# Cutting the last loads of a decode kernel differently: values in two pieces, down weights in four

## The chip, the cores and the metric

The kernel runs on one core of a Trainium2 chip. The metric is device time in microseconds (us) of the whole program, lower is better. A profile is one execution; its span is a little shorter than the device time (512.7 us against about 514.3 us), because it counts from the first to the last recorded instruction. Engines: PE is the matrix engine (PEld its weight loads), DVE the vector engine, ACT the scalar engine, POOL is GpSimd, and SP is the engine that issues nearly all loads.

## The reference, cut to what matters

One token goes through attention and MLP, and then through both once more with the same weights and the same cache. Attention reads the last 4,096 keys and values of 32 heads of width 192; the MLP is 640 to 1,536 and back.

```python
def _A_ref(x, k_cache, v_cache, wq, wo):
    W = min(4096, max(256, Sk // 4))                     # 4096
    q = ... x @ wq ...
    scores = jnp.einsum("bhqd,bhkd->bhqk", q, k) * (Dh ** -0.5)
    p = _softmax(scores, axis=-1)
    o = jnp.einsum("bhqk,bhkd->bhqd", p, v)
    return ... o @ wo
def _B_ref(x, w_gate, w_up, w_down):
    g = x @ w_gate; u = x @ w_up                          # cut: einsums
    return (_sigmoid(g) * u) @ w_down
x = x + _A_ref(_layernorm(x), ...)
x = x + _B_ref(_layernorm(x), ...)
# the same two lines once more
```

For a single token this is a job of moving bytes: 218 MB of cache and weights for a few matrix-vector products.

## The kernel before

Keys and values come in head pairs, through seven slots of on-chip memory. `seq` is the order of loads; SP issues each as soon as its slot is free, so loads are mostly queued well ahead of the compute (about 20 us at the end). The last cache load of a layer is that of the values of one head pair (12,288 columns of 2 bytes on 128 partitions; the first half is head 0, the second head 1). It was cut in three: head 1 as `b1` (in layer 1 with the output weights behind it), then head 0 as two quarters. The matmuls of head 1 run first, then those of each quarter.

```python
def last_values(l, p):
    return [("b1", l, p), ("b0", l, p, 0), ("b0", l, p, 1)]
...
elif k == "b1":
    n, o1 = len(pg.ops["dma"]), UNIT if it[1] else VE
    pg.dma(q_dma(slot(s, NB * DH, o1 - NB * DH), b_in(it[2], NB * DH, o1)), f"b1_{it[1]}", wr=[rslot[s]])
elif k == "b0":
    o = it[3] * NHALF                                     # NHALF: a quarter, 3072 columns
    pg.dma(q_dma(slot(s, o, NHALF), b_in(it[2], o, o + NHALF)), f"bh{it[3]}", wr=[res(f"bh{it[3]}")], extra=ev_done["b1"])
```

In layer 1 the gate, up and down weights of the last MLP follow at once. `finish` ends the program: up projection, then the down projection, whose weights come in `WFIN` pieces, each with its own semaphore.

```python
WFIN = [(0, 6), (6, 10), (10, 12)]                        # blocks of 128 rows of w_down
...
nc.all_engine_barrier()                                   # line 882
finish()                                                  # of which, after the up projection:
for i_, (c0, c1) in enumerate(WFIN):
    if i_ < 2:
        nc.tensor.wait_ge(tail_sem["copy"], i_ + 1)
    for c in range(c0, c1):
        for g in range(NRG):                              # 4 column groups of the PE array
            i = nc.tensor.matmul(yrow[32 * g:32 * g + 1, 0:RW], lhsT=hT[:, c:c + 1],
                                 rhs=slot(D_SLOT, c * D + g * RW, RW), ..., tile_position=(0, 32 * g))
            if c == c0 and g == 0:
                i._wait_ge(tail_sem[f"d:wf{i_}"], 16)
i.then_inc(tail_sem["row"], 1)
nc.vector.tensor_copy(out=o_row[...], in_=yrow[...])._wait_ge(tail_sem["row"], 3).then_inc(tail_sem["copy"], 1)
```

## Time and profile before

| what | before |
|---|---|
| device time, median of the first three runs | 514.38 us (514.02 to 514.49) |
| span of the profile | 512.7 us |
| bytes loaded, mean rate | 218.71 MB, 427 GB/s |
| last landing of a load | 510.05 us |
| last landing to start of the closing copy | 0.53 us |

The head of the profile's page. The rows in tenths give the busy share of each of 40 slices, the GB/s row what the load engines moved in each:

```profile
span 512.7 us, 8581 instructions
...
PE 263.9 (51%) x3716; PEld 138.7 (27%) x3716; DVE 100.3 (20%) x379; ACT 85.0 (17%) x171; POOL 4.2 (1%) x31
...
DMA  9999999999999999999999999999999999999996
GB/s 431 426 423 426 427 430 428 430 461 439 426 430 426 435 430 426 443 457 430 394 420 415 419 438 441 434 425 425 461 439 435 426 426 430 445 426 417 427 429 273
DMA packets 9964, 218.71 MB, mean 427 GB/s; under 512 B 1240, under 2 KB 1368, under 8 KB 4952
```

The load engines are busy in every slice but the last, and no compute engine is busy for much over half the time. What can be won is overhead of transfers, or work left over when the last byte has landed. That work is in the chain of waits (start us, length, what), here of the last microseconds:

```profile
485.35 24.70 DMA big<-in_wd_dram
510.05 0.04 issue
510.10 0.46 PE o L748 x6
510.56 0.02 issue
510.58 0.33 DVE o_sb L754
```

The last down-weight load was issued at 485.35 and landed at 510.05; then come eight matmuls (the chain counts six of them), the copy out of PSUM, and the store. The timeline around the last values of layer 1 (start us, length, engine, line, what; in brackets the idle time before it and what ended it):

```profile
492.69 0.82 PE L487 MATMUL o<-big,et_sb 128*2 128x384 bf16 x16
494.45 0.65 PE L487 MATMUL o<-big,et_sb 128*2 128x384 bf16 x8 [0.94 <-DMA big<-in_uc_dram]
496.30 0.81 PE L487 MATMUL o<-big,et_sb 128*2 128x384 bf16 x8 [1.20 <-DMA big<-in_uc_dram]
...
500.86 1.76 PE L674 MATMUL scores<-sh,big 128*128 128x1 bf16 x60 [0.40 <-DVE sc L372]
505.74 1.07 PE L735 MATMUL scores<-sh,big 128*128 128x1 bf16 x35 [1.82 <-PEq L882]
507.81 0.97 PE L748 MATMUL o<-big,sh 128*1 128x160 bf16 x24 [0.33 <-DMA big<-in_wd_dram]
...
510.09 0.10 PEld L748 LDWEIGHTS o<-big,sh 128*1 128x1 bf16 x8 [0.41 <-DMA big<-in_wd_dram]
```

Head 1 runs at 492.69, the two quarters of head 0 at 494.45 and 496.30, each on its landing. Then the gate projection starts at 500.86, the up projection at 505.74, the down projection at 507.81. The last eight weight loads of PE, at 510.09, wait for the last down-weight piece.

The windows view near the end shows how the load stream runs out (time, length, busy time of PE, PEld, DVE, ACT, POOL, granted PE clock, busy share of the load engines, GB/s):

```profile
507.00:508.00 1.00, 0.67 (x26) 0.58 (x27) 0.30 (x2) 0.00 (x0) 0.00 (x0) 0.50 0.71 289
508.00:509.00 1.00, 0.78 (x24) 0.43 (x16) 0.00 (x0) 0.00 (x0) 0.00 (x0) 0.50 0.48 188
509.00:510.00 1.00, 0.67 (x16) 0.36 (x16) 0.00 (x0) 0.00 (x0) 0.00 (x0) 0.50 0.16 61
```

The sixteen load engines don't finish together (the last load has sixteen landing records, from 507.31 to 510.05 us): the rate falls over three microseconds, and the last of them sets the landing.

### The profile page before, as it was taken

Reading aid. Unit: us, or ns where it says so; the run is one execution under the profiler, and the core shown is the slowest. Engines: PE = TensorE matmul, PEld = TensorE weight load, DVE = VectorE, ACT = ScalarE, POOL = GpSimd, SP = SyncE. Lnnn points to the kernel's source line nnn. Section 1 sums busy time; section 2 is a strip of 40 time slices with the busy share of each in tenths; the row PEclk is TensorE's granted clock in tenths of the full one; section 3 lists DMA queues with packets and bytes.
Section 4 is the critical chain, followed back from the end, with each engine's and each line's share of the span. In section 5 each row is a group of like instructions: output and inputs, shape, how many; then the busy total and the mean of one; then the engine's idle time right before and its main releaser. Section 6 shows DMA issues by size and latency. Waiting matters only on the chain.

```text
span 512.7 us, 8581 instructions
## 1 busy us (share of the span) xinstructions
PE 263.9 (51%) x3716; PEld 138.7 (27%) x3716; DVE 100.3 (20%) x379; ACT 85.0 (17%) x171; POOL 4.2 (1%) x31
## 2 busy tenths in 40 slices
PE   0362455344643254445565777774625344634665
PEld 0221222122312122222234434532312122312334
DVE  0221212112210121112121243321202111210311
ACT  1110111011110111011120024130301011101220
POOL 0010000000000000000000000000000000000000
PEclk9955665566565775556575568765755566556565
DMA  9999999999999999999999999999999999999996
GB/s 431 426 423 426 427 430 428 430 461 439 426 430 426 435 430 426 443 457 430 394 420 415 419 438 441 434 425 425 461 439 435 426 426 430 445 426 417 427 429 273
DMA packets 9964, 218.71 MB, mean 427 GB/s; under 512 B 1240, under 2 KB 1368, under 8 KB 4952
## 3 DMA queue, kind: packets, MB, share of 16 engines
q1 hardware_dynamic: 9800, 218.37, 99.1%
q8 instruction: 13, 0.21, 0.1%
q10 hardware_dynamic: 144, 0.06, 0.0%
q14 instruction: 7, 0.06, 0.0%
HBM read 218.43 MB, written 0.00 MB: 426 GB/s over the span
## 4 chain that ended last, share of the span: by engine, by line
DMA 63%; PE 24%; DVE 7%; ACT 3%; SPq 2%; issue 2%; DVEq 0%; POOL 0%; ACTq 0%; POOLq 0%
DMA big<-in_uc_dram 54%; PE scores L430 8%; PE o L487 7%; DMA big<-in_wd_dram 6%; DMA big<-in_wu_dram 3%; DVE sc L440 3%; PE bank L446 2%; SPq L214 2%; PE bank L412 2%; ACT e_sb L454 2%; PE bank L522 1%; PE bank L460 1%; ACT diag L443 1%; DVE sc L472 1%; DVE qs L418 1%
## 5 line engine op out<-in xcount | busy, mean ns | idle before, releaser
L430 PE MATMUL scores<-big,qs 128*32 128x512 bf16 x744 | 82.9, 613 | 10.3 <-DVE qs L418 9.6
L412 PE MATMUL bank<-sh,big 128*128 128x1 bf16 x465 | 17.1, 166 | 132.5 <-DMA big<-in_uc_dram 130.1
L487 PE MATMUL o<-big,et_sb 128*2 128x384 bf16 x1024 | 78.1, 471 | 5.4 <-DMA big<-in_uc_dram 4.2
L443 ACT ACTIVATE diag<-cst,sc 128x128 f32<-128x128 bf16 x32 | 12.8, 401 | 307.9 <-DVE sc L440 292.3
L440 DVE TENSOR_REDUCE sc<-scores 128x1 f32<-128x1024 f32 x31 | 37.9, 1224 | 78.9 <-PE scores L430 78.9
L412 PEld LDWEIGHTS bank<-sh,big 128*128 128x128 bf16 x465 | 14.7, 104 | 135.6 <-DMA big<-in_uc_dram 113.4
L446 PE MATMUL bank<-diag,sc 128*128 128x128 f32 x64 | 22.7, 452 | 47.2 <-ACT diag L443 47.2
L454 ACT ACTIVATE e_sb<-scores,sc 128x1024 bf16<-128x1024 f32 x31 | 37.3, 1204 | 42.1 <-DVE sc L449 39.7
L487 PEld LDWEIGHTS o<-big,et_sb 128*2 128x2 bf16 x1024 | 28.6, 108 | 42.1 <-issue 29.8
L418 DVE TENSOR_TENSOR qs<-bank,cst 128x96 bf16<-128x96 f32 x30 | 7.7, 258 | 162.5 <-PE bank L412 162.5
L430 PEld LDWEIGHTS scores<-big,qs 128*32 128x32 bf16 x744 | 24.4, 133 | 43.8 <-issue 31.4
L446 PEld LDWEIGHTS bank<-diag,sc 128*128 128x128 f32 x64 | 14.2, 277 | 72.3 <-ACT diag L443 71.1
L494 ACT CAST o_sb<-o 128x384 bf16<-128x384 f32 x64 | 29.8, 473 | 21.2 <-PE o L487 21.0
L522 PE MATMUL bank<-sh,big 128*128 128x1 bf16 x480 | 17.1, 165 | 15.1 <-DVE sh L511 14.7
L464 DVE CAST et_sb<-bank 128x64 bf16<-128x64 f32 x32 | 7.2, 225 | 70.2 <-PE bank L460 70.2
L522 PEld LDWEIGHTS bank<-sh,big 128*128 128x128 bf16 x480 | 14.5, 99 | 17.6 <-DVE sh L511 12.3
L447 DVE TENSOR_REDUCE sc<-bank 128x2 f32<-128x128 f32 x32 | 9.3, 292 | 41.9 <-PE bank L446 41.9
L460 PEld LDWEIGHTS bank<-cst,e_sb 128*128 128x128 bf16 x256 | 8.9, 101 | 22.8 <-issue 16.3
L460 PE MATMUL bank<-cst,e_sb 128*128 128x8 bf16 x256 | 11.7, 169 | 6.6 <-ACT e_sb L454 6.5
L470 PE MATMUL o<-sc 128*128 128x2 f32 x62 | 13.8, 292 | 0.6 <-ACT o_sb L494 0.6
L470 PEld LDWEIGHTS o<-sc 128*128 128x128 f32 x62 | 11.9, 240 | 1.9 <-ACT o_sb L494 1.3
L472 DVE RECIPROCAL sc<-o 64x1 f32<-64x1 f32 x62 | 10.2, 164 | 9.4 <-PE o L470 7.7
(78 smaller groups left out, 107.8 us busy)
## 6 DMA issues: line engine op xcount, KB each, us to landing
big<-in_uc_dram SPq DMA_DIRECT2D x20, 7104.0 KB, 22.6
big<-in_uc_dram SPq DMA_DIRECT2D x11, 3552.0 KB, 21.4
big<-in_uc_dram SPq DMA_DIRECT2D x2, 3072.0 KB, 18.0
big<-in_uc_dram SPq DMA_DIRECT2D x7, 480.0 KB, 6.6
big<-in_uc_dram SPq DMA_DIRECT2D x4, 768.0 KB, 11.6
big<-in_uc_dram SPq DMA_DIRECT2D x1, 2048.0 KB, 11.1
big<-in_uc_dram SPq DMA_DIRECT2D x1, 2016.0 KB, 10.4
big<-in_wg_dram SPq DMA_DIRECT2D x4, 480.0 KB, 14.6
```

Source lines behind the costliest of these rows:

```text
L412: ins = t.matmul(qe[:, i:i + 1], lhsT=w[:, c * 2 * DH + c0:c * 2 * DH + c0 + P], rhs=xq[:, c:c + 1], start=(c == 0), stop=(c == DC - 1))
L430: ins = t.matmul(sc_x[1 + b][32 * j:32 * j + 32, :], lhsT=qs[:, y, k, :], rhs=slot(sa, WQE + k * W + (4 * b + j) * 512, 512), start=(k == ...
L440: pg.op("dve", lambda v: v.reduce_max(out=mx, in_=sc_x[0][:], axis=AX.X), wr=[res("mx")], ex=sc_x[3:5])
L443: pg.op("act", lambda a: a.mul(out=diag[:], in_=ident, mul=mx), rd=[res("cst"), res("mx")], wr=[res("diag")])
L446: pg.op("pe", lambda t: t.matmul(dmx[:, 0:P], lhsT=ones_f, rhs=diag[:], start=True, stop=True), rd=[res("diag"), res("ones")], ex=[rb[2]])
L454: pg.op("act", lambda a: a.activation(out=e_sb[:], in_=sc_x[0][:], func=ACT.Exp, bias=nbias, scale=srs_c, accum_out=rowsum), rd=[res("nbia ...
L460: ins = t.matmul(qe[:, 0:2 * NB].rearrange("p (r x) -> p r x", r=2)[:, :, 4 * b:4 * b + 4], lhsT=e_sb[:, b * P:(b + 1) * P], rhs=sel, star ...
L470: pg.op("pe", lambda t: t.matmul(sm, lhsT=ones_f, rhs=rs2[z], start=True, stop=True), rd=[res(f"rs2{z}"), res("ones")], wr=[res("rsum")], ...
L472: rb[bk].last["dve"] = pg.op("dve", lambda v, h=h: v.reciprocal(out=Rn[z][64 * h:64 * h + 64], in_=sm[64 * h:64 * h + 64, h:h + 1]), rd=[r ...
L487: ins = t.matmul(o8[h][32 * j:32 * j + 2, 0:2 * DH].rearrange("p (a d) -> p a d", a=2), lhsT=et_sb[:, z, h * NB + 2 * u:h * NB + 2 * u + 2 ...
L494: pg.op("act", lambda a, h=h: a.copy(out=o8_sb[:, :, h * DH:(h + 1) * DH], in_=o8[h][:, 0:2 * DH].rearrange("p (a d) -> p a d", a=2)), wr= ...
L522: ins = t.matmul(yT[:, j:j + 1], lhsT=wo[:, c * D + j * P:c * D + (j + 1) * P], rhs=oTb[z][:, c:c + 1], start=False, stop=(c == 2), skip_g ...
```

## The change

It does two things. The last values come as a piece of three quarters (head 1 and the second half of head 0) and a final quarter, so there is one transfer fewer in each layer. The last down weights come in four pieces, the last of one block, so that four matmuls instead of eight are left when the last piece lands.

```diff
-    WFIN = [(0, 6), (6, 10), (10, 12)]
+    WFIN = [(0, 6), (6, 10), (10, 11), (11, 12)]
@@
-        return [("b1", l, p), ("b0", l, p, 0), ("b0", l, p, 1)]
+        return [("b1", l, p), ("b0", l, p)]
@@
-    seq += [("fg",), ("fu",), ("fd", 0), ("fd", 1), ("fd", 2)]
+    seq += [("fg",), ("fu",), *(("fd", i) for i in range(len(WFIN)))]
@@
-            pg.dma(q_dma(slot(s, NB * DH, o1 - NB * DH), b_in(it[2], NB * DH, o1)), f"b1_{it[1]}", wr=[rslot[s]])
+            pg.dma(q_dma(slot(s, NHALF, o1 - NHALF), b_in(it[2], NHALF, o1)), f"b1_{it[1]}", wr=[rslot[s]])
@@
-            o = it[3] * NHALF
-            pg.dma(q_dma(slot(s, o, NHALF), b_in(it[2], o, o + NHALF)), f"bh{it[3]}", wr=[res(f"bh{it[3]}")], extra=ev_done["b1"])
+            pg.dma(q_dma(slot(s, 0, NHALF), b_in(it[2], 0, NHALF)), "bh0", wr=[res("bh0")], extra=ev_done["b1"])
@@
-                for part in (0, 1) if half and h == 0 else (None,):
+                for part in (1, 0) if half and h == 0 else (None,):
...                 (which matmuls start and stop the PSUM group follows the new order)
```

More of the change, by code (lines that the diff above doesn't have):

```diff
@@ L480, in PVmm, with f @@
                 vt = (mreg(h * NB * DH, NB * DH) if inm else slot(sv, v_at(p) + h * NB * DH, NB * DH)).rearrange("p (t d) -> p t d", t=NB)
-                for part in (0, 1) if half and h == 0 else (None,):
+                for part in (1, 0) if half and h == 0 else (None,):
                     us = range(NB // 2) if part is None else range(part * NB // 4, (part + 1) * NB // 4)
-                    def f(t, h=h, vt=vt, us=us):
+                    first = range(NB // 4, NB // 4 + 4) if part is not None else range(4)
+                    final = range(NB // 4 - 4, NB // 4) if part is not None else range(NB // 2 - 4, NB // 2)
+                    def f(t, h=h, vt=vt, us=us, first=first, final=final):
                         for u in us:
@@ L487, in f @@
                             ins = t.matmul(o8[h][32 * j:32 * j + 2, 0:2 * DH].rearrange("p (a d) -> p a d", a=2), lhsT=et_sb[:, z, h * NB + 2 * u:h * NB + 2 * u + 2],
-                                           rhs=vt[:, 2 * u:2 * u + 2, :], start=(u < 4), stop=(u >= NB // 2 - 4), tile_position=(0, 32 * j))
+                                           rhs=vt[:, 2 * u:2 * u + 2, :], start=u in first, stop=u in final, tile_position=(0, 32 * j))
                         return ins
-                    rV = rc if inm else [rslot[sv]] + ([] if part is None else [res(f"bh{part}")]) if half else [rval[sv]]
+                    rV = rc if inm else [rslot[sv]] + ([res("bh0")] if part == 0 else []) if half else [rval[sv]]
                     ev = pg.op("pe", f, rd=[res(f"et{z}")] + rV, ex=[rb[4 + h]])
```

## The prediction

> **What bounds the kernel.** One stream of loads, from the first microsecond to 510. The page's first lines give 218.71 MB in a span of 512.7 us, mean 427 GB/s; in its slices the DMA engines are at 9 tenths or more in every slice but the last, while PE is busy 51%, DVE 20%, ACT 17% of the span. The Trainium skill, "DMA: Bandwidth & Descriptors", Specifications, gives 435 GB/s as the fabric ceiling; the trace agrees (427), so only fewer bytes, less overhead per transfer, or a shorter end can help. Bytes don't change.
>
> **The two places touched.**
>
> 1. Last values (layer 0 at 258-271 us, layer 1 at 482-497 us). Timeline: the last 8 value matmuls wait for the final 768 KB piece and start at 269.98 and 496.30. The new final piece has the same size, position and number of matmuls behind it, so it should land at the same time. Three quarters now arrive together, so 24 matmuls run when the larger piece lands, near 494.4 in layer 1 rather than 16 at 492.7 and 8 at 494.45: about 1.3 us of work in a gap of 1.85 us, hidden. Nor is the end of these stages critical: in layer 0 the next step waits for output weights behind the values (272.5), in layer 1 for the gate weights (500.86), which the stream delivers when it will. One issue fewer saves about 0.43 us of the SP queue per layer (chain of waits: 0.42-0.49 us each), but the queue is about 20 us ahead of the data, so that is worth nothing.
>
> 2. Last down weights. The chain of waits ends with a load until 510.05, 0.46 us of PE (8 matmuls, two rounds of four column groups), a 0.33 us DVE copy, the store. With a last piece of one block only 4 matmuls follow the last landing. Two rounds take 0.46 and 24 matmuls (six rounds) take 0.97, so a round is about 0.13 us: estimated gain 0.13 us, all on the critical path. The block before it lands about 0.38 us earlier and is done by then.
>
> **Overhead of transfers.** Packet records: 2,560-byte rows take 102 ns each, 56,832-byte rows 2,099 ns; at the long rows' rate 2,560 bytes would take 95, so a packet costs 7-8 ns beyond its bytes. An engine carries 8 rows of each transfer: one transfer more costs about 0.07 us of stream, one fewer saves as much. Two are removed, one is added: net about -0.07 us, an estimate. The same skill page ("Why a DMA increments its semaphore by 16 and not by 1") says that a load's engines finish independently; here the windows show the rate falling to 289, 188 and 61 GB/s in 507-510 us, so the last landing belongs to the slowest engines, and splitting doesn't rebalance them.
>
> **Sum.** 514.38 - 0.13 - 0.07 = about 514.2 us, less than the spread of the three runs (514.02 to 514.49). Range 513.7 to 514.7. Within 2%: 0.985; faster 0.005; slower 0.01.
>
> **What would show it.** The chain still ends with the down-weight load, landing at 510.0 within 0.15; the group of last matmuls after it near 0.33 us instead of 0.46, 4 of them waiting; the last value matmuls still starting near 270 and 496.2; the gate projection near 500.8; mean DMA rate unchanged within 1 GB/s.
>
> **What would make it wrong.** A hiccup per small transfer (1,280-byte rows) larger than 8 ns per packet, which would land the last piece late; a different skew among the 16 engines; the queue filling up so that the issue of a later load stalls; or the larger value piece delaying matmuls enough to push the layer norm behind the gate weights (slack about 0.1 us in layer 1). Each is under 1 us.

## The result, and the profile after

| | before | after |
|---|---|---|
| device time, median of 6 runs each | 514.29 us | 514.03 us |
| ratio, 95% interval | | 0.9992 (0.9976 to 1.0007) |
| span of the profile | 512.7 us | 512.7 us |
| transfers' packets | 9964 | 9820 |
| last landing | 510.05 us | 510.24 us |
| last landing to closing copy | 0.53 us | 0.40 us |

The ratio isn't quite that of the medians. The interval holds 1, and the difference of the medians, 0.26 us, is smaller than the spread of either kernel. One of the six runs of before took 516.20 us; the mean of the other five is 514.24, against 514.14 of the changed kernel.

The head of the page of the changed kernel, and below it the end of its chain of waits:

```profile
span 512.7 us, 8580 instructions
...
DMA packets 9820, 218.71 MB, mean 427 GB/s; under 512 B 1224, under 2 KB 1608, under 8 KB 4808
```

```profile
484.55 24.91 DMA big<-in_wd_dram
509.45 0.04 issue
509.50 1.12 PE o L749 x24
510.62 0.02 issue
510.64 0.33 DVE o_sb L755
```

Bytes and rate are unchanged. The chain now follows the matmuls back through the two last pieces without a break, so it names the landing at 509.45; the timeline (PEld, the weight loads, shows the wait best) has the last four matmuls wait for the last piece:

```profile
507.97 0.97 PE L749 MATMUL o<-big,sh 128*1 128x160 bf16 x24 [0.40 <-DMA big<-in_wd_dram]
...
510.28 0.09 PEld L749 LDWEIGHTS o<-big,sh 128*1 128x1 bf16 x4 [0.29 <-DMA big<-in_wd_dram]
510.64 0.33 DVE L755 CAST o_sb<-o 97x160 bf16<-97x160 f32 x1 [2.81 <-PE o L749]
```

The landing records put the last landing at 510.24, so 0.40 us pass until the copy instead of 0.53. But the last landing itself came 0.19 us later than in before, and that hides the 0.13 us saved behind it: 0.06 of it stood already at the landing of the up weights (505.45 against 505.39), and the down weights took 4.79 us from there instead of 4.66. Of these 0.13, 0.10 are in the first down piece (2.48 instead of 2.37 us), which the change doesn't touch; the repeats below show that this is scatter. Around the last values:

```profile
494.52 2.73 PE L488 MATMUL o<-big,et_sb 128*2 128x384 bf16 x32 [1.80 <-DMA big<-in_uc_dram]
...
496.02 0.48 ACT L495 CAST o_sb<-o 128x384 bf16<-128x384 f32 x1 [4.64 <-PE o L488]
...
500.97 1.75 PE L675 MATMUL scores<-sh,big 128*128 128x1 bf16 x60 [0.79 <-DVE o L664]
505.83 1.07 PE L736 MATMUL scores<-sh,big 128*128 128x1 bf16 x35 [1.82 <-PEq L883]
```

Twenty-four matmuls start at 494.52, on the landing of the larger piece, and run into the last eight, whose quarter landed at 496.38. The gate projection starts 0.11 us later than before, as its weights land (500.92 against 500.82).

### The profile page after: what moved, and what is told of

Its sections match the earlier page's. It is cut to its first block, busy times and chain, and to the rows that moved or that the text cites. A ratio compares the mean times of both kernels' runs of the same rounds, so it can differ in the third digit from the quotient of the medians.

```text
span 512.7 us, 8580 instructions
## 1 busy us (share of the span) xinstructions
PE 260.9 (51%) x3716; PEld 136.9 (27%) x3716; DVE 100.4 (20%) x379; ACT 84.8 (17%) x171; POOL 4.2 (1%) x31
## 2 busy tenths in 40 slices
DMA packets 9820, 218.71 MB, mean 427 GB/s; under 512 B 1224, under 2 KB 1608, under 8 KB 4808
## 4 chain that ended last, share of the span: by engine, by line
DMA 63%; PE 23%; DVE 7%; ACT 3%; issue 2%; SPq 2%; DVEq 0%; POOL 0%; ACTq 0%; POOLq 0%
DMA big<-in_uc_dram 54%; PE scores L429 9%; PE o L488 7%; DMA big<-in_wd_dram 6%; DMA big<-in_wu_dram 3%; DVE sc L439 3%; PE bank L445 2%; PE bank L411 2%; SPq L214 2%; ACT e_sb L453 2%; PE bank L523 1%; PE bank L459 1%; ACT diag L442 1%; DVE sc L471 1%; PE o L469 1%
## 5 line engine op out<-in xcount | busy, mean ns | idle before, releaser
L488 PE MATMUL o<-big,et_sb 128*2 128x384 bf16 x1024 | 76.1, 465 | 6.1 <-DMA big<-in_uc_dram 3.6
L488 PEld LDWEIGHTS o<-big,et_sb 128*2 128x2 bf16 x1024 | 27.8, 106 | 41.7 <-issue 28.6
L459 PEld LDWEIGHTS bank<-cst,e_sb 128*128 128x128 bf16 x256 | 9.0, 101 | 23.9 <-issue 17.4
```

The costliest lines, as they stand in the source:

```text
L459: ins = t.matmul(qe[:, 0:2 * NB].rearrange("p (r x) -> p r x", r=2)[:, :, 4 * b:4 * b + 4], lhsT=e_sb[:, b * P:(b + 1) * P], rhs=sel, star ...
L488: ins = t.matmul(o8[h][32 * j:32 * j + 2, 0:2 * DH].rearrange("p (a d) -> p a d", a=2), lhsT=et_sb[:, z, h * NB + 2 * u:h * NB + 2 * u + 2 ...
```

## The experiments

The main theory: the change is worth 0.13 us, one round of four matmuls behind the last landing; the values and the number of transfers are worth next to nothing. The rivals: the values carry what difference there is; or there is none at all. All runs gave correct results. Times are medians of five runs, ratios are to the kernel before on the same chip (nine runs), each with an interval of about plus or minus 0.0013, so the traces decide more than the times. "Tail" means last landing to closing copy.

### The kernel before against itself

> The kernel before, unchanged, against itself: how far two medians and two profiles of one kernel lie apart. Expected: ratio within 0.0005 of 1, last landing within 0.3 us between profiles, last landing to closing copy 0.53 us with less than 0.03 us of scatter.

Measured: 514.43 us against 514.22, ratio 1.0001. Tail 0.53 us, as in the first profile. The last landing was at 510.62 instead of 510.05, so one kernel's landing moved by 0.57 us between two profiles: more than expected, and four times the effect under study. Differences of times below about 0.5 us say nothing here; the tail, which repeats to 0.01 us, does.

### Each part alone

```diff
# e1_tail_only: kernel before, and
-    WFIN = [(0, 6), (6, 10), (10, 12)]
+    WFIN = [(0, 6), (6, 10), (10, 11), (11, 12)]
...                 (the loads follow len(WFIN), as in the change; so in the next two)
# e2_values_only: changed kernel, and
-    WFIN = [(0, 6), (6, 10), (10, 11), (11, 12)]
+    WFIN = [(0, 6), (6, 10), (10, 12)]
```

> Only the down weights in four pieces, values as before. Main theory (the gain is matmuls taken from behind the last landing): from the last landing to the start of the closing DVE copy 0.40 us as in the changed kernel instead of 0.53, four matmuls behind the last landing; stream 0.07 us longer for one more transfer; in all about 0.06 us under before (ratio near 0.9999). Rival (the values are where the 0.26 us between the medians comes from): ratio 1.0000 or above in the time, though the tail is shorter. Rival (nothing but noise): can be told by the trace only, not by these times.

> Only the values in two pieces of three quarters and one quarter, down weights in three pieces as before. Main theory: tail after the last landing 0.53 us as before with eight matmuls; the gate projection starts at the landing of the gate weights, within 0.2 us of before; stream shorter by at most 0.14 us for two transfers fewer; ratio 0.9997 to 1.0000. Rival (the values carry the gain): ratio near 0.9995 and a gate projection that starts 0.2 us or more earlier, counted from the first landing of the run.

Measured: the tail alone 514.27 us, ratio 0.9993, tail 0.40 us; the values alone 514.29 us, ratio 0.9997, tail 0.53 us (before: 514.56). The shorter tail goes with the down weights, as the main theory has it. With the values alone the gate projection started at 501.06, 490.05 us after the first landing, against 489.89 in before: not earlier, so the rival that the values carry a gain is gone. The times don't separate the two parts.

### More and fewer matmuls behind the last landing

```diff
# e4_tail_two: kernel before, and
-    WFIN = [(0, 6), (6, 10), (10, 12)]
+    WFIN = [(0, 6), (6, 12)]
# e5_tail_twelve: kernel before, and
-    WFIN = [(0, 6), (6, 10), (10, 12)]
+    WFIN = [(i, i + 1) for i in range(12)]
```

> Down weights in two pieces of six blocks, so 24 matmuls (six rounds) behind the last landing. Main theory: last landing to closing copy about 1.05 us instead of 0.53 (four rounds more of 0.13), one transfer fewer saves 0.07: +0.45 us, ratio about 1.0009. Rival (time at the end is set by something other than the matmuls behind the last landing): no change.

> Down weights in twelve pieces of one block: nine transfers more than before at the end. Main theory with my size of 0.07 us a transfer: last landing 0.63 us later, last landing to closing copy 0.40 us instead of 0.53: +0.5 us, ratio about 1.001. Rival (a transfer costs nothing beyond its bytes): last landing unchanged, total -0.13 us, ratio 0.9997. Rival (small transfers hiccup by more than their packets): over +1 us.

Two pieces: 514.74 us, ratio 1.0005; tail 1.07 us, within 0.02 of what was expected. The chain of waits of this run:

```profile
484.70 25.60 DMA big<-in_wd_dram
510.30 0.04 issue
510.34 1.00 PE o L748 x14
511.34 0.02 issue
511.37 0.33 DVE o_sb L754
```

Six rounds take 1.07 us from landing to copy, two take 0.53, one takes 0.40: 0.13 us a round (at a granted clock of 0.50 in all three, as the windows above show it for 507 to 510 us) and about 0.27 us that stay. This is the mechanism of the change, shown over three sizes.

Twelve pieces: 514.41 us, ratio 0.9998; tail 0.40 us. The chain ends the same way, with four matmuls:

```profile
510.63 0.04 issue
510.67 0.33 PE o L748 x4
511.00 0.02 issue
511.03 0.33 DVE o_sb L754
```

Single blocks landed 0.40 to 0.46 us apart, 0.41 in the middle; in the kernel before a pair of blocks in one transfer took 0.76. Two blocks thus took 0.82 us in two transfers, 0.06 more than in one. The engine that finishes first gives a little less: from its part of the up weights to its part of the last down piece it took 5.05 us instead of 4.67, 0.04 for each of the nine transfers more. A single transfer more can't be seen: with the last pair cut in two, as in the change, it took 0.75 to 0.79 us in four profiles. By the last engine the whole of the down weights took 4.99 us after the up weights, between the two profiles of the kernel before (4.66 and 5.11). So my 0.07 was too high, and whether the expected loss of 0.5 us came in part can't be told from the time, whose interval (0.9984 to 1.0011) reaches from a gain of 0.8 us to a loss of 0.6. A hiccup of over 1 us is ruled out by it.

### The price of a transfer in the middle of the stream

```diff
# e6_values_many: kernel before, and
-            pg.dma(q_dma(slot(s, o, NHALF), b_in(it[2], o, o + NHALF)), f"bh{it[3]}", wr=[res(f"bh{it[3]}")], extra=ev_done["b1"])
+            n = NHALF // 8
+            for c in range(8):
+                pg.dma(q_dma(slot(s, o + c * n, n), b_in(it[2], o + c * n, o + c * n + n)), f"bh{it[3]}",
+                       wr=[res(f"bh{it[3]}")] if c == 7 else [], extra=ev_done["b1"])
```

> Each of the two quarter pieces of values in eight transfers (768 bytes a row), 28 transfers more in all, matmuls as before. Main theory with my size of 0.07 us a transfer: +2.0 us in the stream, ratio about 1.004; last values landing about 1.0 us later, counted from the landing before them. Rival (a transfer costs nothing beyond its bytes): no change. Rival (the queue fills and the issues stall): more than +2 us, with long issues on the SP queue.

Measured: 515.89 us, ratio 1.0031 (1.0018 to 1.0045), the first clear loss. 0.0031 of 514 us is 1.6 us for 28 transfers more, 0.057 each, with rows of 768 bytes. In layer 1, from the landing of the pair before to that of the last value, it took 9.10 us instead of 8.49: 0.044 for each of 14. The queue did fill: 17 issues took 11.35 us, and two of them 2.43 and 1.87 us (at 485.94 and 488.41) where most take 0.43. But the busy share of the load engines stayed at 0.95 to 1.17 from 490 to 498 us, and the loss is below the 2 us of that rival. So a transfer has a price and it comes out in the time; with 0.04 to 0.06 us, here and for the rows of 1,280 bytes, my 0.07 was some 20% to 75% too high. Taking one away, as the change does, moved this stretch from 8.49 us (8.50 in the repeat) to 8.49 (8.47 in the repeat and with the values alone): nothing that can be seen. In the two runs with one piece, below, it took 8.38 us; the engine that lands first shows less of that (8.47 and 8.41 us, against 8.47 and 8.49 in the two profiles of before).

### How late may the values be?

```diff
# e3_values_one: from e2_values_only, the values in one piece
-        return [("b1", l, p), ("b0", l, p)]
+        return [("b1", l, p)]
-            pg.dma(q_dma(slot(s, NHALF, o1 - NHALF), b_in(it[2], NHALF, o1)), ...
+            pg.dma(q_dma(slot(s, 0, o1), b_in(it[2], 0, o1)), ...
-                for part in (1, 0) if half and h == 0 else (None,):
+                for part in (None,):
# e7_one_and_four: the same, but with WFIN = [(0, 6), (6, 10), (10, 11), (11, 12)]
# e9_values_half: kernel before, head 0 in one piece instead of two quarters
-        return [("b1", l, p), ("b0", l, p, 0), ("b0", l, p, 1)]
+        return [("b1", l, p), ("b0", l, p, 0)]
-    NHALF = NB * DH // 2
+    NHALF = NB * DH
...                 (and the matmuls of head 0 in one part)
```

> The last values of each layer in one piece, down weights as before: 32 matmuls behind the landing instead of 8, so the end of attention moves about 1.9 us later in both layers. Main theory (the end of the values is hidden behind the stream: gate weights, then up weights): gate projection of layer 1 starts up to 2 us later, but the up projection still starts when its weights land (near 505.7) and the time is the same, ratio 0.9995 to 1.0003. Rival, as the prediction had it (slack only about 0.1 us in layer 1): +1.8 us, ratio 1.0035.

> Values in one piece and down weights in four. Main theory: as the changed kernel less two more transfers, ratio to before about 0.9995, tail 0.40 us. Rival (slack of the values too small): above 1.003.

Measured: one piece 515.02 us, ratio 1.0010 (0.9997 to 1.0024); one piece with four down pieces 514.92 us, ratio 1.0012 (0.9998 to 1.0025), tail 0.73 us instead of the expected 0.40. Both my theory (no cost) and its rival (1.8 us) missed: by ratios and medians it costs 0.5 to 0.8 us, though each interval alone still holds 1. The chain of waits of the one-piece run shows why. It holds no load at the end:

```profile
508.45 1.07 PE scores L736 x35
509.53 0.67 PE o L736 x25
510.19 1.73 PE o L749 x48
511.92 0.02 issue
511.95 0.33 DVE o_sb L755
```

The last landing was at 510.98, but the copy came at 511.95: the matmuls of the down projection ran in one go, 48 of them from 510.12 on by the timeline, without waiting for weights. The up projection starts 4.85 us after the gate projection (503.60 to 508.45), in the kernel before 4.88 us (500.86 to 505.74): it waits behind the barrier of all engines that stands ahead of `finish` (the profile names PE's own sequencer, at line 882, the barrier), not for its weights, which had landed at 505.39 in the kernel before and at 506.27 in this run, 2.18 us before it started. So a late end of attention moves gate, up and down alike. From these numbers one can work out how late it may be. In this run the first down matmul came 1.67 us after the up projection, and the copy 1.83 us after that. With the gate at 500.86 that is 500.86 + 4.88 + 1.67 + 1.83 = 509.24 us, and the copy of the kernel before started at 510.58: a slack of about 1.3 us. The single piece moved the gate by 2.74 us, of which 1.4 is over the slack, as 511.95 - 510.58 = 1.37 shows. A later run was to confirm it:

> Last values in two pieces of one half each: 16 matmuls behind the landing instead of 8, about 0.65 us more. Main theory after the one-piece run (about 1.3 us of slack between the end of the values and the last matmuls, because the down weights are waited for later): gate projection about 0.6 us later than in before, counted from the landing of the last values (5.2 us instead of 4.6), but the last matmuls still wait for the last landing, tail 0.53 us, ratio 0.9995 to 1.0003. Rival (every delay of the values' end comes out at the end, beyond 0.1 us): +0.55 us, ratio 1.0010, closing copy no longer right behind the last landing.

Measured: 514.41 us, ratio 1.0005 (0.9991 to 1.0018). The gate projection started 5.21 us after the landing of the last values (496.12 to 501.33) instead of 4.60, and the tail was 0.53 us: the closing copy was right behind the last landing, as the slack of 1.3 us says. The ratio alone, 0.0002 outside of what was expected, can't decide between the two; the tail does.

### The changed kernel again, and the scatter

> The changed kernel a second time. Main theory: last landing to closing copy 0.40 us again with four matmuls behind the landing; the time of the last landing itself scatters by up to 0.6 us between profiles, by whether the 16 KB instruction fetch near 504.6 us falls on the slowest DMA engine; ratio to before 0.9990 to 1.0000. Rival (the shorter tail was scatter): a tail above 0.45 us.

Measured: 514.32 us against 514.48, ratio 0.9998; tail 0.40 us with four matmuls; last landing 510.67, that is 0.43 us later than in its first profile. The tail repeats, the landing doesn't. The landing records of the kernel before show where its landing moved between two profiles. Between the landings of the up weights and of the first down piece, the two last engines of its first profile took 2.35 and 2.37 us (505.38 to 507.73, 505.39 to 507.76). In the repeat the second-last took 2.35 (505.45 to 507.80), but the last 2.86 (505.50 to 508.36). In both an instruction fetch of 16,384 bytes, recorded with 0.93 us, ran at 504.5 to 504.7. The records don't name the engine that a packet ran on, so that the fetch hit the slowest engine in the repeat is inferred. It isn't what delayed the repeat of the changed kernel: there the last engine took 2.30 us over the same stretch (2.48 in the first profile), and the landing of the pair before the last values was already 0.55 us later (488.43 against 487.88). So the theory, that this one fetch decides the landing, doesn't hold for the run that it was made for. The last experiment adds fetches on purpose:

```diff
# e10_more_fetches: kernel before with a tile `idle`, after each of the 26 small POOL memsets that mark a landing
+        for _ in range(60):
+            pg.op("pool", lambda g: g.memset(idle[0:1, 0:1], 0.0), wr=[res("idle")], own="idle")
```

> The kernel before with some 1,560 one-element memsets more on the otherwise idle POOL engine, nothing waits for them. Theory (an instruction fetch of 16 KB takes 0.6 us of one of the 16 load engines, which never catches up, and the slowest engine sets the end): about six fetches more ([...]an estimate from 13 fetches for 8,581 instructions would give two), each putting one engine 0.6 us behind: spread of the last landing above 3.4 us or last landing 0.3 to 2 us later, ratio 1.0005 to 1.004. Rival (fetches are absorbed): spread and last landing as in the other profiles of before (2.7 to 3.3 us; 510.0 to 510.7), ratio within 0.0005 of 1.

Measured: 519.24 us, ratio 1.0093 (1.0079 to 1.0107): 4.8 us slower, for work that almost nothing waits for (one copy on POOL stands behind the first sixty memsets, at 36.83 instead of 27.86 us, and PE waits 1.6 us for it). Lines of its page (busy time by engine; load queues with packets, MB and share), and the end of its chain of waits:

```profile
PE 258.5 (50%) x3716; PEld 136.5 (26%) x3716; DVE 100.5 (19%) x379; ACT 84.7 (16%) x171; POOL 141.8 (27%) x1591
...
q8 instruction: 13, 0.21, 0.1%
q14 instruction: 19, 0.16, 0.1%
```

```profile
515.57 0.04 issue
515.61 0.47 PE o L751 x8
516.08 0.02 issue
516.10 0.32 DVE o_sb L757
```

The added instructions show as 12 more fetch packets of 8 KB on the fetch queue (19 instead of 7, at 0.309 us each), a tenth of a megabyte of 218, or 63 bytes for each added instruction. The chain still ends with a load and a tail of 0.53 us; the last landing moved from 510.05 to 515.57. From one landing to the next the big loads take 16.7 us, but 17.4 in six places (164.0, 198.1, 232.3, 407.7, 441.8 and 476.0 us), where the kernel before has 16.7 to 16.8 each time, with a recorded fetch in each of these gaps (fetches at 118.3, 173.8 and 451.6 us left no such gap), and the first and the last engine drift apart from 1.8 us (at 146.6) to 4.1 us (at 258). This fits fetches that are paid for by single load engines, of which the slowest sets the pace. The lag doesn't stay with them: the first engine was only 0.13 us later than in before at 253.9, but 3.05 us at 299.6. In between, from 278 to 284 us, the rate was 317 GB/s (before: 414); loads there are issued only 3 to 5 us before they begin to land, once PE frees their slots, and PE waits for the last engine, so that the late engine held up the others is inferred. Six gaps of 0.65 us more are 3.9 of the 5.5 us; the rest isn't accounted for, nor that a gap grew by 0.65 us for a packet of 0.309, and the busy POOL itself isn't told apart from its fetches by this run.

## Why the prediction was right

- **The time.** 514.2 us was predicted, 514.03 measured. The range would also have held the kernel before, and that the medians fell by about the 0.2 us of the sum is luck within the scatter, so the hit of the time proves little; the steps matter.
- **The bound.** The stream of loads at 427 GB/s was the bound and stayed it: bytes and rate are unchanged to the last digit.
- **Matmuls behind the last landing.** "Estimated gain 0.13 us, all on the critical path": measured 0.13 (0.53 to 0.40), the same in all four profiles with a last piece of one block that weren't held up by late values, and 0.13 a round in the run with two pieces. Right in kind and size.
- **"One transfer more costs about 0.07 us ... net about -0.07 us".** Here a size was off. I took a packet's recorded time above its bytes (7 to 8 ns) for lost time of the stream. The recorded times of neighbouring packets overlap: rows of 2,560 bytes have records of 102 ns, but two blocks land in 0.76 us, and an eighth of that, one row of each engine, is 95 ns. Rows of 1,280 bytes have 55 ns, and a block lands in 0.41 us, 51 ns a row, where the long rows' rate gives 47: only half of the excess was lost time. Measured: 0.04 to 0.06 us for a transfer more, and no gain to be seen for one removed. The net term of the change, two less and one more, is within the scatter.
- **"About 1.3 us of work in a gap of 1.85 us, hidden".** Hidden, but by little. Cut this way PE idles for 1.80 us before the larger piece, and the first 16 of its matmuls took about 1.5 us (494.52 to the copy that waits for them at 496.02), where the same 16 took 0.82 before. The windows view gives the granted clock as 1.00 for 492 to 494 us in before, and in the changed kernel:

```profile
494.00:495.00 1.00, 0.48 (x8) 0.24 (x12) 0.00 (x0) 0.00 (x0) 0.00 (x0) 0.63 1.10 467
495.00:496.00 1.00, 1.00 (x20) 0.42 (x12) 0.00 (x0) 0.00 (x0) 0.00 (x0) 0.50 1.03 439
```

  The Trainium skill, "TensorE: Matmul & The Clock Gate", Part 1, says that the clock of PE falls to half after an idle window of about 3.4 us and that the window runs freely, so the point of the change varies. This case agrees in the halved clock and in the varying point (in the repeat of the kernel before, 492 to 494 us had 0.75). It doesn't show the idle window: the trace's clock records have the full clock from 490.85 to 494.26 and half of it from there to 497.68, each 3.41 us long, but PE worked until 492.73, so the clock fell after 1.5 us of standing still, and what the halving was decided on stays open. Matmuls were costed at the wrong clock; it cost nothing, because of the slack.
- **"Slack about 0.1 us in layer 1".** Too small, though nothing hung on it in the change itself. 0.1 us is the distance to the gate weights; what counts is the distance to the end, and that is about 1.3 us from the start of the gate projection (the one-piece and half-piece runs). My later belief that the values' end was hidden without limit, because the up projection waits for its weights, was wrong as well: it waits at the barrier.
- **"Landing at 510.0 within 0.15".** It was 510.24, and 510.67 in the repeat. The landing itself scatters by 0.6 us between profiles of one kernel, which the prediction should have allowed for.

## What to carry to other kernels

In a kernel that is bound by its loads, what cutting pieces differently can win is mostly what follows the last landing: count the rounds of matmuls behind it (0.13 us each here), and set against it what the transfers added cost in the stream (0.04 to 0.06 us each here). Before cutting or merging anything earlier, measure how late that stage may be (1.3 us here), since within that slack a later end costs nothing. When an effect is a quarter of the scatter of the time, look for an interval of the trace that repeats, and enlarge the effect in an experiment until it stands out.

## What the Trainium skill lacked or had wrong

- "DMA: Bandwidth & Descriptors", Where 436 GB/s comes from: it says that the HBM side, about 358 GB/s, binds transfers between HBM and on-chip memory. Here one core loaded 218.71 MB from HBM at 427 GB/s over the whole span, near the page's own fabric ceiling of 435. The page's section Measured has it right (425 GB/s for 16 MB with one core, about 358 only when both cores of a pair stream); the sentence lacks that condition.
- The same page, Measured, has 341 GB/s for a transfer of 1 MB issued from GpSimd and calls transfers under 64 KB dominated by descriptors. It gives no price of one transfer more inside a queue of SP that never runs empty. Here that was 0.04 to 0.06 us (rows of 1,280 and of 768 bytes), and pieces of 163,840 bytes landed every 0.41 us, about 400 GB/s.
- "Runtime: NRT & Kernel Launch", Instruction fetch mechanics, calls the cost of crossing a fetch block mostly hidden. It doesn't say whether in a kernel bound by loads a fetch takes time of the load stream. The runs suggest it and don't prove it: 12 fetch packets more (and a busy POOL) came with 4.8 us more, and a fetch is a possible cause of 0.5 us by which the last landing of the kernel before moved.
- No page says how far the load engines come apart over one long stream. In the kernel before, first and last engine were 0.5 us apart at the first landings and 2.7 us at the last, so that the rate fell to 289, 188 and 61 GB/s in the last three microseconds. It came in two steps, between the landings at 27.8 and 45.8 us (0.49 to 1.79) and at 327.3 and 337.0 us (1.64 to 2.92); between the two it stayed between 1.4 and 2.0 us.
